# Attention, a polynomial layer and an expert layer on one core: the keys' and queries' work of the pair two on queued behind the reciprocal

## The chip, the cores and the metric

One core of one Trainium2 chip runs the whole program in one launch. The metric is the device time of one execution in microseconds (us); lower is better. The time before is the median of three runs, 1173.3 us (1172.96 to 1173.52).

## The reference

Four batches of eight heads, 768 positions, 64 numbers a head, float32. Attention sees the first four positions (sinks) and a window of 128 behind each position. Its output goes through two layers in turn.

```python
scores = where(keep, q @ k.T / 8, -1e9)          # keep: sink, or 0 <= i - j < 128
a = exp(scores - max); a = a / (sum(a) + 1e-9)
x = (a @ v) as 3072 x 512                        # heads side by side
h = x @ w_in                                     # 512 -> 2048
g = h if h >= 1, 0 if h <= -1, else (h + 1)**2 / 4
x2 = g @ w_out                                   # 2048 -> 512
logits = x2 @ w_gate                             # 8 experts, 384 tokens each
out[mask_e] = relu(x2[mask_e] @ w1[e]) @ w2[e]   # tokens given out greedily by logit
```

## The kernel before

**Work and stages.** Tokens are cut into 12 blocks of 256 (`NB`), three to a batch, so every third block is a batch's first. A block's attention is done in four pairs of heads. Blocks 0 and 1 take a float32 path (`attn_steps_f32`); blocks 2 to 11, so 40 pairs, take `attn_steps`, in which each operand is split into a high and a low part and multiplied in several passes. Beside the attention of one block runs the first layer of the block before it (`moe1_steps`): 16 steps of 12 matmuls into `hp` (L632), the activation on VectorE (L640, L642), ScalarE (L641, L643) and GpSimd (`gl`, L644), and 12 matmuls into `up` (L657). From some 60 to 780 us both run together; after that come the routing and the experts. A function `Plan` sorts all steps by a due time and traces them in that order; a scheduler then orders each engine's queue, and may issue an instruction earlier than another traced before it when it is ready sooner. Each queue is worked off in order.

**One pair.** In the tracing order of `pipeline` (L598) an iteration does, for the pair called `now`, the one after it (`+`), the pair two on (`*`) and three on (`^`):

```python
"ptrans0 ptrans1 strans +s00 +s01 +norm0 pv0 +s10 +s11 +norm1 "
"*trans_k *trans_q ^load_kq "
"pv1 +split_v +sinks *load_v split"
```

- `scores` (s00 to s11): TensorE multiplies queries and keys (L332 with the queries' low part `ql`, L333 with the high part `sq`); VectorE adds the mask and takes the maximum (L335, two instructions); ScalarE takes the exponential and its row sum (L337, the sum in a second record).
- `norm`: VectorE adds 1e-9 to the sums (L342) and takes the reciprocal (L343); GpSimd multiplies the probabilities `pr` by it (L351; L346 and L348 in a batch's first block).
- `ptrans`: TensorE turns `pr` (L370) into `tp`; ScalarE and VectorE make the high and low part `pt` (L372, L373).
- `pv`: TensorE (L389); ScalarE copies one half of the result (L395), VectorE adds the other into `xa` (L396). `split`: GpSimd adds the two parts of `xa` (L408; L405 in a first block), ScalarE makes `xh` (L409), GpSimd `xl` (L410). With the fourth pair's `xh` and `xl` a block's input is complete, and the matmuls of L632 on that block can start.
- `trans_k`, for the pair two on: VectorE turns the keys in place (L428, called through `turned`), ScalarE copies the high part into `ks` (L300) and VectorE subtracts it (L301), one for each head; VectorE copies the sinks' keys (L305 in a first block, L306).
- `trans_q`, for the pair two on: VectorE turns the queries (L428), ScalarE makes `sq` (L314), VectorE `ql` (L315).
- `load_kq`, for the pair three on: SyncE loads keys and queries (L424) into the buffers that `trans_k` and `trans_q` read.

Keys `kr` and queries `qr`, `ks`, `sq` and `ql` have one buffer each; `pr`, `pt` and `sm` have two.

Of the kernel before, what the change touches and what calls it, by code (L numbers as in the profile page):

```python
# [1 line left out]

# [5 lines left out]
F32 = mybir.dt.float32  # L8
F32R = mybir.dt.float32r
# [3 lines left out]
AF = mybir.ActivationFunctionType  # L13
OP = mybir.AluOpType
# [11 lines left out]
P = 128  # L26
NT = S // P
NS = 32
# [46 lines left out]
class Kernel:  # L75
# [174 lines left out]
    def attn_steps(self, blk, xt):  # L250

        nc, a = self.nc, self.a
        pairs = []
        b, t0 = blk // BB, 2 * (blk % BB)
        first = t0 == 0
        kts = [0, 1] if first else [t0 - 1, t0, t0 + 1]
        nk = len(kts)
        for p in range(H // 2):
            st = {}
# [34 lines left out]
            half = [(slice(64 * hh, 64 * hh + 64), slice(64 - 64 * hh, 128 - 64 * hh)) for hh in range(2)]  # L294

            def trans_k(p=p, st=st):
                ks = st["ks"] = self.at.tile([P, 2, 3, W], F32R, name="ks", tag="ks")
                ps = self.turned(st["k"][:, :4 * nk].rearrange("p n c -> p (n c)")).rearrange("p (t c) -> p t c", c=P)
                for hh, (hs, os) in enumerate(half):
                    nc.scalar.copy(ks[hs, hh, :nk, :P], ps[hs])  # L300
                    nc.vector.tensor_tensor(out=ks[os, hh, :nk, :P], in0=ps[hs], in1=ks[hs, hh, :nk, :P].bitcast(F32),  # L301
                                            op=OP.subtract)
                if first:
                    self.sk[p] = self.kp.tile([P, 2, NS], F32R, name="sk", tag=f"sk{p}")
                    nc.vector.tensor_copy(self.sk[p], ks[:, :, 0, :NS].bitcast(F32))  # L305
                nc.vector.tensor_copy(ks[:, :, :nk - 1, P:],  # L306
                                      self.sk[p].bitcast(F32).unsqueeze(2).to_broadcast([P, 2, nk - 1, NS]))

            def trans_q(st=st):
                sq = st["sq"] = self.at.tile([P, 2, 2, P], F32R, name="sq", tag="sq")  # L310
                ql = st["ql"] = self.at.tile([P, 2, 2, P], F32R, name="ql", tag="ql")
                x = self.turned(st["q"].rearrange("p h n c -> p (h n c)"))
                flat = lambda t: t.rearrange("p h u q -> p (h u q)")
                nc.scalar.activation(flat(sq), x, AF.Copy, scale=0.125)  # L314
                nc.vector.scalar_tensor_tensor(flat(ql), x, 0.125, flat(sq).bitcast(F32), op0=OP.mult, op1=OP.subtract)  # L315

            def scores(hh, u, st=st):
                t = t0 + u
# [21 lines left out]
            def norm(hh, st=st):  # L340
                pr, sm = st["pr"][:, :, :, hh], st["sm", hh]
                nc.vector.tensor_scalar(sm[:, 2], sm[:, 1], 1e-9, None, op0=OP.add)  # L342
                nc.vector.reciprocal(sm[:, 2], sm[:, 2])  # L343
                r = sm[:, 2]
                if first:
                    nc.gpsimd.tensor_tensor(out=pr[:, 0, W:], in0=pr[:, 0, W:], in1=r[:, 0:1].to_broadcast([P, P]),  # L346
                                            op=OP.mult)
                    nc.gpsimd.tensor_tensor(out=pr[:, 1], in0=pr[:, 1], in1=r[:, 1:2].to_broadcast([P, 2 * P + NS]),  # L348
                                            op=OP.mult)
                else:  # L350
                    nc.gpsimd.tensor_tensor(out=pr, in0=pr, in1=r.unsqueeze(2).to_broadcast([P, 2, 2 * P + NS]),  # L351
                                            op=OP.mult)
# [45 lines left out]
            def split(p=p, st=st):  # L398
# [7 lines left out]
                else:  # L406
# [4 lines left out]

            pairs.append(dict(
                load_kq=load_kq, load_v=load_v, trans_k=trans_k, trans_q=trans_q,
                split_v=vsplit, sinks=sinks if first else None, strans=None if first else strans, split=split,
                **{f"s{hh}{u}": lambda hh=hh, u=u, f=scores: f(hh, u) for hh in range(2) for u in range(2)},
                **{f"{nm}{hh}": lambda hh=hh, f=f: f(hh) for hh in range(2)
                   for nm, f in (("norm", norm), ("ptrans", ptrans), ("pv", pv))}))
        return pairs

    def load_blocks(self, t, src, ts):  # L420

        for j in range(2):
            blocks = src[ts[0] * P:(ts[-1] + 1) * P, 32 * j:32 * j + 32].rearrange("(n s) d -> s n d", s=32)
            self.nc.sync.dma_start(t[32 * j:32 * j + 32, :4 * len(ts)], blocks)  # L424

    def turned(self, x):

        self.nc.vector.transpose(x, x)  # L428
        return x
# [946 lines left out]
def tile_sink_window_attention__moe__expert_choice(ctx, tc, q, k, v, n_sink, window, w_in, w_out, wg, w1, w2, out):  # L1376
    a = dict(q=q, k=k, v=v, n_sink=n_sink, window=window, w_in=w_in, w_out=w_out, wg=wg, w1=w1, w2=w2, out=out)
    nc = tc.nc
    K = Kernel(ctx, tc, a)
# [3 lines left out]
    xg = dr.tile([B * H * S, D], F32, name="xg")  # L1383
    K.logits = K.c.tile([P, B * NT, E], F32, name="logits")
    K.sk, K.sv, K.skf, K.svf = {}, {}, {}, {}

    def pipeline(general):
        with ExitStack() as c0:
            c1, c3, c4, cd = (c0.enter_context(ExitStack()) for _ in range(4))
            K.pools(c1.enter_context, c0.enter_context)  # L1390
# [72 lines left out]
            plan.run()  # L1463

    pipeline(False)
    flag = nc.values_load(K.flag[0:1, 0:1], min_val=0, max_val=1)
    with tc.If(flag):
        with ExitStack() as c0:
            K.attn_general(c0.enter_context, xg)
        pipeline(True)  # L1470
# [32 lines left out]
```

## Time and profile before

| | |
|---|---|
| profiled execution | 1172.83 us, of which the span of the profile is 1171.0 us |
| median of the runs | 1173.3 us |
| TensorE (PE) busy | 1102.2 us, 94% of the span |
| VectorE (DVE) busy | 872.2 us, 74% |
| ScalarE (ACT) busy | 698.2 us, 60% |
| GpSimd (POOL) busy | 487.0 us, 42% |
| granted TensorE clock, mean | 0.982 of full |

The profile is one execution. An engine's busy time leaves out register, branch, semaphore and DMA-issuing instructions. Matmuls are pipelined, so a busy TensorE is not one at its peak. In a row in order of time stand the start, the duration, the engine, the line of the kernel, the operation, the tiles written and read, their shapes, the count, and in brackets the engine's idle time before it and what ended it. A wait for several things is put down to the last of them.

### The profile page before, as it was taken

What the parts mean: (1) busy time and instruction counts of PE and PEld (TensorE: products, weight loads), DVE (VectorE), ACT (ScalarE), POOL (GpSimd) and SP (SyncE); (2) the same over time, 40 slices, a digit from 0 to 9 for tenths busy, and PEclk for the clock granted to TensorE, in tenths of its full rate; (3) what the DMA queues carried; (4) which work ended last, traced back from release to release, by engine and by line L of the source; (5) the groups of instructions that cost most, each with busy time, mean ns of one, the idle gap of its engine ahead of it and who ended that gap; (6) DMA issues with size and microseconds to landing.
All of it is one profiled execution on the core that took longest, in us unless ns stands there. A gap on an engine that the chain in (4) does not pass through costs nothing.

```text
span 1171.0 us, 24367 instructions
## 1 busy us (share of the span) xinstructions
PE 1102.2 (94%) x8256; PEld 1017.4 (87%) x8256; DVE 872.2 (74%) x2718; ACT 698.2 (60%) x1598; POOL 487.0 (42%) x590
## 2 busy tenths in 40 slices
PE   5899888999999999999999999999799999999997
PEld 3688878999999999999999999999587788788896
DVE  5978978777777877776777787755788888788430
ACT  4887777566666666676667676643245445444552
POOL 1335745444545545455545554542213213322321
PEclk9899999999999999999999999999799999999999
DMA  4645522323222222223222222100485767667772
GB/s 105 173 143 158 158 60 61 70 42 64 53 39 56 36 55 49 61 46 64 34 54 49 58 46 56 22 19 1 120 228 168 204 180 216 188 194 202 217 218 66
DMA packets 241928, 118.13 MB, mean 101 GB/s; under 512 B 196096, under 2 KB 220672, under 8 KB 241792
## 3 DMA queue, kind: packets, MB, share of 16 engines
q1 hardware_dynamic: 231504, 85.36, 28.4%
q0 software_dynamic: 8592, 29.89, 10.9%
q8 instruction: 67, 1.10, 0.4%
q10 hardware_dynamic: 1696, 1.22, 0.3%
q14 instruction: 69, 0.57, 0.2%
HBM read 86.00 MB, written 13.11 MB: 85 GB/s over the span
## 4 chain that ended last, share of the span: by engine, by line
PE 42%; DVE 13%; issue 9%; ACT 6%; POOL 5%; DMA 4%; SPq 2%; DVEq 0%; POOLq 0%; ACTq 0%
PE hp L632 11%; PE up L657 11%; PE hp L1048 6%; PE us L1075 6%; PE xp L389 1%; DVE oh L945 1%; ACT pr L337 1%; ACT u L641 1%; PE tp L370 1%; SPq L424 1%; DVE u L640 1%; DVE ind L801 1%; DVE ks L301 1%; DMA qr<-in_q_dram 1%; POOL gl L644 1%
## 5 line engine op out<-in xcount | busy, mean ns | idle before, releaser
L644 POOL TENSOR_TENSOR gl<-u,gh 128x256 fp32r<-128x256 f32 x192 | 149.5, 779 | 205.3 <-ACT gh L643 169.5
L657 PE MATMUL up<-woh,gl 128*128 128x256 f32 x576 | 166.6, 289 | 2.6 <-POOL gl L644 2.6
L657 PE MATMUL up<-woh,gh 128*128 128x256 f32 x576 | 163.7, 284 | 0.0
L657 PE MATMUL up<-wol,gh 128*128 128x256 f32 x576 | 163.5, 284 | 0.0
L641 ACT ACTIVATE u<-u,half 128x256 f32<-128x256 f32 x192 | 97.4, 508 | 83.4 <-DVE u L640 79.4
L632 PE MATMUL hp<-xh,wil 128*128 128x256 f32 x768 | 132.0, 291 | 3.6 <-ACT xh L409 2.8
L632 PE MATMUL hp<-xl,wih 128*128 128x256 f32 x768 | 126.4, 284 | 2.0 <-POOL xl L410 1.6
L632 PE MATMUL hp<-xh,wih 128*128 128x256 f32 x768 | 124.7, 283 | 0.0
L632 PEld LDWEIGHTS hp<-xh,wil 128*128 128x128 f32 x768 | 107.6, 191 | 5.7 <-ACT xh L409 4.2
L657 PEld LDWEIGHTS up<-woh,gl 128*128 128x128 f32 x576 | 108.9, 189 | 3.2 <-POOL gl L644 3.1
L632 PEld LDWEIGHTS hp<-xl,wih 128*128 128x128 f32 x768 | 106.4, 191 | 3.4 <-POOL xl L410 3.4
L657 PEld LDWEIGHTS up<-wol,gh 128*128 128x128 f32 x576 | 108.6, 189 | 0.4 <-issue 0.4
L657 PEld LDWEIGHTS up<-woh,gh 128*128 128x128 f32 x576 | 108.5, 188 | 0.4 <-issue 0.4
L632 PEld LDWEIGHTS hp<-xh,wih 128*128 128x128 f32 x768 | 106.3, 191 | 0.0
L642 DVE TENSOR_TENSOR u<-hp,u 128x256 f32<-128x256 f32 x192 | 80.5, 420 | 31.6 <-ACT u L641 29.8
L640 DVE TENSOR_SCALAR u<-hp 128x256 f32<-128x256 f32 x192 | 79.9, 416 | 31.0 <-PE hp L632 22.5
L351 POOL TENSOR_TENSOR pr<-pr,sm 128x576 f32<-128x576 f32 x56 | 71.3, 1273 | 67.9 <-DVE sm L343 30.3
L643 ACT CAST gh<-u 128x256 fp32r<-128x256 f32 x192 | 77.6, 404 | 30.3 <-DVE u L642 28.0
L337 ACT ACTIVATE pr<-pr,sm 128x288 f32<-128x288 f32 (+1 forms) x160 | 85.2, 533 | 16.3 <-DVE sm L335 15.7
L1056 ACT ACTIVATE hh<-hp 128x384 fp32r<-128x384 f32 x64 | 31.5, 492 | 102.1 <-PE hp L1048 89.4
L373 DVE TENSOR_TENSOR pt<-tp,pt 128x512 fp32r<-128x512 f32 (+1 forms) x80 | 51.3, 647 | 43.9 <-ACT pt L372 43.4
L1075 PE MATMUL us<-w2h,hl 128*128 128x512 f32 x192 | 80.8, 421 | 0.0
(264 smaller groups left out, 3040.0 us busy)
## 6 DMA issues: line engine op xcount, KB each, us to landing
w1r<-in_moe_w_dram SPq DMA_DIRECT2D x32, 512.0 KB, 4.7
w2r<-in_moe_w_dram SPq DMA_DIRECT2D x32, 512.0 KB, 4.5
w2l<-w2r POOLq DMA_DIRECT2D x32, 512.0 KB
qr<-in_q_dram SPq DMA_DIRECT2D x320, 32.0 KB, 1.9
dr<-in_moe_w_in_dram SPq DMA_DIRECT2D x15, 512.0 KB, 4.1
dr<-in_moe_w_out_dram SPq DMA_DIRECT2D x15, 512.0 KB, 3.7
x2d<-ev SPq DMA_DIRECT2D x26, 256.0 KB, 2.2
vr<-in_v_dram SPq DMA_DIRECT2D x56, 96.0 KB, 2.3
```

What stands on the lines that cost most here:

```text
L337: nc.scalar.activation(pr, pr, AF.Exp, bias=sm[:, 0, u:u + 1], scale=-1.0, accum_out=sm[:, 1, u:u + 1])
L351: nc.gpsimd.tensor_tensor(out=pr, in0=pr, in1=r.unsqueeze(2).to_broadcast([P, 2, 2 * P + NS]), op=OP.mult)
L373: nc.vector.tensor_tensor(out=pt[:, 1, :n], in0=ps, in1=pt[:, 0, :n].bitcast(F32), op=OP.subtract)
L632: nc.tensor.matmul(ps, w_[:, k, fs], x_[:, k, :], start=(i == 0 and k == 0), stop=(i == 2 and k == 3))
L640: nc.vector.tensor_scalar(u, ps, -1.0, 1.0, op0=OP.max, op1=OP.min)
L641: nc.scalar.activation(u, u, AF.Square, bias=self.half, scale=0.5)
L642: nc.vector.tensor_tensor(out=u, in0=ps, in1=u, op=OP.max)
L643: nc.scalar.copy(gh, u)
L644: nc.gpsimd.tensor_tensor(out=gl, in0=u, in1=gh.bitcast(F32), op=OP.subtract)
L657: nc.tensor.matmul(o, g_[:, ts], self.w_out_part(w_, f)[:, cs], start=(f == fa and i == 0 and (cs.start > 0 or t == 0)), stop=(f == fz - 1 ...
L1048: nc.tensor.matmul(ps, w_[:, k, fs], x_[:, k, :], start=(i == 0 and k == 0), stop=(i == 2 and k == 3))
L1075: nc.tensor.matmul(us[j], h_[:, o], w_[:, f % 2, :], start=(f == 0 and i == 0), stop=(f == nf - 1 and i == 2))
```

## The change

A helper, `behind_shares`, opens a block in which every instruction traced for VectorE gets an order edge to the last reciprocal of `norm` traced so far (`self.shares`). Such an edge fixes the order of issue on that engine's queue and waits for nothing else. `trans_k` opens the block after the keys' transposition, `trans_q` around everything. By the tracing order that reciprocal is the one of the next pair's second head (`+norm1`), traced right before. ScalarE's instructions in the block get no edge. The instructions are the same in kind and number. The float32 path does not change.

```diff
--- before.py
+++ after.py
@@ -1,4 +1,4 @@
-from contextlib import ExitStack
+from contextlib import ExitStack, nullcontext
 
 import concourse.bass as bass
 import concourse.tile as tile
@@ -296,23 +296,26 @@
             def trans_k(p=p, st=st):
                 ks = st["ks"] = self.at.tile([P, 2, 3, W], F32R, name="ks", tag="ks")
                 ps = self.turned(st["k"][:, :4 * nk].rearrange("p n c -> p (n c)")).rearrange("p (t c) -> p t c", c=P)
-                for hh, (hs, os) in enumerate(half):
-                    nc.scalar.copy(ks[hs, hh, :nk, :P], ps[hs])
-                    nc.vector.tensor_tensor(out=ks[os, hh, :nk, :P], in0=ps[hs], in1=ks[hs, hh, :nk, :P].bitcast(F32),
-                                            op=OP.subtract)
-                if first:
-                    self.sk[p] = self.kp.tile([P, 2, NS], F32R, name="sk", tag=f"sk{p}")
-                    nc.vector.tensor_copy(self.sk[p], ks[:, :, 0, :NS].bitcast(F32))
-                nc.vector.tensor_copy(ks[:, :, :nk - 1, P:],
-                                      self.sk[p].bitcast(F32).unsqueeze(2).to_broadcast([P, 2, nk - 1, NS]))
+                with self.behind_shares():
+                    for hh, (hs, os) in enumerate(half):
+                        nc.scalar.copy(ks[hs, hh, :nk, :P], ps[hs])
+                        nc.vector.tensor_tensor(out=ks[os, hh, :nk, :P], in0=ps[hs], in1=ks[hs, hh, :nk, :P].bitcast(F32),
+                                                op=OP.subtract)
+                    if first:
+                        self.sk[p] = self.kp.tile([P, 2, NS], F32R, name="sk", tag=f"sk{p}")
+                        nc.vector.tensor_copy(self.sk[p], ks[:, :, 0, :NS].bitcast(F32))
+                    nc.vector.tensor_copy(ks[:, :, :nk - 1, P:],
+                                          self.sk[p].bitcast(F32).unsqueeze(2).to_broadcast([P, 2, nk - 1, NS]))
 
             def trans_q(st=st):
                 sq = st["sq"] = self.at.tile([P, 2, 2, P], F32R, name="sq", tag="sq")
                 ql = st["ql"] = self.at.tile([P, 2, 2, P], F32R, name="ql", tag="ql")
-                x = self.turned(st["q"].rearrange("p h n c -> p (h n c)"))
                 flat = lambda t: t.rearrange("p h u q -> p (h u q)")
-                nc.scalar.activation(flat(sq), x, AF.Copy, scale=0.125)
-                nc.vector.scalar_tensor_tensor(flat(ql), x, 0.125, flat(sq).bitcast(F32), op0=OP.mult, op1=OP.subtract)
+                with self.behind_shares():
+                    x = self.turned(st["q"].rearrange("p h n c -> p (h n c)"))
+                    nc.scalar.activation(flat(sq), x, AF.Copy, scale=0.125)
+                    nc.vector.scalar_tensor_tensor(flat(ql), x, 0.125, flat(sq).bitcast(F32),
+                                                   op0=OP.mult, op1=OP.subtract)
 
             def scores(hh, u, st=st):
                 t = t0 + u
@@ -340,7 +343,7 @@
             def norm(hh, st=st):
                 pr, sm = st["pr"][:, :, :, hh], st["sm", hh]
                 nc.vector.tensor_scalar(sm[:, 2], sm[:, 1], 1e-9, None, op0=OP.add)
-                nc.vector.reciprocal(sm[:, 2], sm[:, 2])
+                self.shares = nc.vector.reciprocal(sm[:, 2], sm[:, 2]).ins
                 r = sm[:, 2]
                 if first:
                     nc.gpsimd.tensor_tensor(out=pr[:, 0, W:], in0=pr[:, 0, W:], in1=r[:, 0:1].to_broadcast([P, P]),
@@ -422,6 +425,10 @@
         for j in range(2):
             blocks = src[ts[0] * P:(ts[-1] + 1) * P, 32 * j:32 * j + 32].rearrange("(n s) d -> s n d", s=32)
             self.nc.sync.dma_start(t[32 * j:32 * j + 32, :4 * len(ts)], blocks)
+
+    def behind_shares(self):
+
+        return self.tc.issue_after(self.shares) if self.shares else nullcontext()
 
     def turned(self, x):
 
@@ -1383,8 +1390,10 @@
     xg = dr.tile([B * H * S, D], F32, name="xg")
     K.logits = K.c.tile([P, B * NT, E], F32, name="logits")
     K.sk, K.sv, K.skf, K.svf = {}, {}, {}, {}
+    K.shares = None
 
     def pipeline(general):
+        K.shares = None
         with ExitStack() as c0:
             c1, c3, c4, cd = (c0.enter_context(ExitStack()) for _ in range(4))
             K.pools(c1.enter_context, c0.enter_context)
```

Below, the issue order at three places, before and in the change. The line numbers in the change are higher: L343 became L346, L342 L345, L301 L302, L306 L307, L305 L306, L315 L317, L335 L338, L428 L435, L396 L399, L373 L376, L640 L647, L642 L649, L590 L597, L351 L354, L644 L651, L408 L411, L410 L413.

VectorE around the second reciprocal of the last pair but one of the last block (at 744 us of the profile), before:

```order
L335 ISA pr,sm<-sc,m_109 128x288
L335 ISA sm 128x1
L301 TENSOR_TENSOR ks<-kr,ks 64x3x128
L642 TENSOR_TENSOR u<-hp,u 128x256
L306 CAST ks<-sk 128x2x2x32
L342 TENSOR_SCALAR sm<-sm 128x2
L428 STREAM_TRANSPOSE qr<-qr 128x512
L343 RECIPROCAL sm<-sm 128x2
L301 TENSOR_TENSOR ks<-kr,ks 64x3x128
L396 TENSOR_TENSOR xa<-xp,xa 64x512
L315 SCALAR_TENSOR_TENSOR ql<-qr,sq 128x512
L373 TENSOR_TENSOR pt<-tp,pt 128x512
```

and in the change:

```order
L338 ISA pr,sm<-sc,m_109 128x288
L338 ISA sm 128x1
L649 TENSOR_TENSOR u<-hp,u 128x256
L345 TENSOR_SCALAR sm<-sm 128x2
L346 RECIPROCAL sm<-sm 128x2
L302 TENSOR_TENSOR ks<-kr,ks 64x3x128 x2
L307 CAST ks<-sk 128x2x2x32
L435 STREAM_TRANSPOSE qr<-qr 128x512
L399 TENSOR_TENSOR xa<-xp,xa 64x512
L376 TENSOR_TENSOR pt<-tp,pt 128x512
L317 SCALAR_TENSOR_TENSOR ql<-qr,sq 128x512
L647 TENSOR_SCALAR u<-hp 128x256
```

Both subtractions of the keys (`ks<-kr,ks`), the copy of the sinks and the queries' transposition stand behind the reciprocal; the step into the reciprocal follows `u` directly. `ql` stands behind the first `pt`.

GpSimd at the same place; the second row of the multiplication of `pr` is the one that this reciprocal releases. Before:

```order
L644 TENSOR_TENSOR gl<-u,gh 128x256 x2
L351 TENSOR_TENSOR pr<-pr,sm 128x576
L644 TENSOR_TENSOR gl<-u,gh 128x256 x2
L351 TENSOR_TENSOR pr<-pr,sm 128x576
L408 TENSOR_TENSOR xa<-xa 128x2x128
L287 TENSOR_TENSOR v_11277<-vr,v_11277 128x6x64
L410 TENSOR_TENSOR xl<-xa,xh 128x256
```

and in the change:

```order
L651 TENSOR_TENSOR gl<-u,gh 128x256 x2
L354 TENSOR_TENSOR pr<-pr,sm 128x576
L651 TENSOR_TENSOR gl<-u,gh 128x256
L354 TENSOR_TENSOR pr<-pr,sm 128x576
L651 TENSOR_TENSOR gl<-u,gh 128x256
L287 TENSOR_TENSOR v_11068<-vr,v_11068 128x6x64
L411 TENSOR_TENSOR xa<-xa 128x2x128
L413 TENSOR_TENSOR xl<-xa,xh 128x256
```

One `gl` that stood ahead of that multiplication now stands behind it, and a split of V (`v<-vr,v`, under its buffer's number) stands ahead of the sum of `xa`.

VectorE around the second reciprocal of the first pair of a batch's third block (at 449 us), before:

```order
L335 ISA pr,sm<-sc,m_108 128x288
L335 ISA sm 128x1
L306 CAST ks<-sk 128x2x2x32
L301 TENSOR_TENSOR ks<-kr,ks 64x3x128 x2
L640 TENSOR_SCALAR u<-hp 128x256
L342 TENSOR_SCALAR sm<-sm 128x2
L343 RECIPROCAL sm<-sm 128x2
L428 STREAM_TRANSPOSE qr<-qr 128x512
L642 TENSOR_TENSOR u<-hp,u 128x256
L396 TENSOR_TENSOR xa<-xp,xa 64x384
L315 SCALAR_TENSOR_TENSOR ql<-qr,sq 128x512
L373 TENSOR_TENSOR pt<-tp,pt 128x384
```

and in the change:

```order
L338 ISA pr,sm<-sc,m_108 128x288
L338 ISA sm 128x1
L647 TENSOR_SCALAR u<-hp 128x256
L345 TENSOR_SCALAR sm<-sm 128x2
L346 RECIPROCAL sm<-sm 128x2
L302 TENSOR_TENSOR ks<-kr,ks 64x3x128 x2
L649 TENSOR_TENSOR u<-hp,u 128x256
L307 CAST ks<-sk 128x2x2x32
L435 STREAM_TRANSPOSE qr<-qr 128x512
L399 TENSOR_TENSOR xa<-xp,xa 64x384
L376 TENSOR_TENSOR pt<-tp,pt 128x384
L317 SCALAR_TENSOR_TENSOR ql<-qr,sq 128x512
```

The copy of the sinks and both subtractions moved from ahead of the reciprocal to behind it, and `xa` and `pt` now stand ahead of `ql`.

VectorE around the second reciprocal after the last pair of a block (at 590 us), before:

```order
L335 ISA pr,sm<-sc,m_108 128x288
L335 ISA sm 128x1
L301 TENSOR_TENSOR ks<-kr,ks 64x2x128 x2
L305 CAST sk<-ks 128x64
L342 TENSOR_SCALAR sm<-sm 128x2
L306 CAST ks<-sk 128x2x32
L640 TENSOR_SCALAR u<-hp 128x256
L343 RECIPROCAL sm<-sm 128x2
L315 SCALAR_TENSOR_TENSOR ql<-qr,sq 128x512
L642 TENSOR_TENSOR u<-hp,u 128x256
L396 TENSOR_TENSOR xa<-xp,xa 64x512
```

and in the change:

```order
L338 ISA pr,sm<-sc,m_108 128x288
L338 ISA sm 128x1
L345 TENSOR_SCALAR sm<-sm 128x2
L346 RECIPROCAL sm<-sm 128x2
L647 TENSOR_SCALAR u<-hp 128x256
L302 TENSOR_TENSOR ks<-kr,ks 64x2x128 x2
L649 TENSOR_TENSOR u<-hp,u 128x256
L306 CAST sk<-ks 128x64
L435 STREAM_TRANSPOSE qr<-qr 128x512
L307 CAST ks<-sk 128x2x32
L399 TENSOR_TENSOR xa<-xp,xa 64x512
L317 SCALAR_TENSOR_TENSOR ql<-qr,sq 128x512
```

Ahead of `xa` stood `ql` and one `u` after the reciprocal; now two `u`, both subtractions, both copies and the queries' transposition stand there.

## Rows read from the trace of the kernel before

**Rows 1.** Table of waits, TensorE, 220 to 780 us: us in total, times, longest.

```profile
PE tp L370 <- POOL pr L351: 12.7, 10, 2.0
PE hp L632 <- ACT xh L409: 2.8, 5, 1.5
PE hp L632 <- POOL xl L410: 1.6, 2, 1.2
PE tp L370 <- POOL pr L346: 1.0, 1, 1.0
PE tp L370 <- POOL pr L348: 0.7, 2, 0.5
```

**Rows 2.** In order of time, 743.9 to 748 us: start, duration, engine, line, operation.

```profile
744.01 0.18 ACT L337 ACTIVATION_READ_ACCUMULATOR pr<-pr,sm 128x1 f32 x1
...
744.20 0.22 DVE L306 CAST ks<-sk 128x128 fp32r<-128x128 f32 x1
...
744.60 0.71 DVE L428 STREAM_TRANSPOSE qr<-qr 128x512 f32<-128x512 f32 x1
...
745.24 0.12 DVE L343 RECIPROCAL sm<-sm 128x2 f32<-128x2 f32 x1
745.29 0.74 POOL L644 TENSOR_TENSOR gl<-u,gh 128x256 fp32r<-128x256 f32 x1 [3.10 <-issue]
...
745.99 1.47 POOL L351 TENSOR_TENSOR pr<-pr,sm 128x576 f32<-128x576 f32 x1
...
747.51 0.75 PE L370 MATMUL tp<-ident,pr 128*128 128x128 f32 x4 [1.07 <-POOL pr L351]
```

**Rows 3.** In order of time, 295.1 to 300.1 us.

```profile
295.11 0.19 ACT L337 ACTIVATION_READ_ACCUMULATOR pr<-pr,sm 128x1 f32 x1
...
295.53 0.17 DVE L343 RECIPROCAL sm<-sm 128x2 f32<-128x2 f32 x1
...
295.73 0.55 DVE L301 TENSOR_TENSOR ks<-kr,ks 64x384 fp32r<-64x384 f32 x1
...
295.84 1.47 POOL L351 TENSOR_TENSOR pr<-pr,sm 128x576 f32<-128x576 f32 x1 [1.18 <-DVE sm L343]
...
296.57 1.15 DVE L301 TENSOR_TENSOR ks<-kr,ks 64x384 fp32r<-64x384 f32 x1 [0.29 <-ACT ks L300]
...
297.75 1.12 DVE L315 SCALAR_TENSOR_TENSOR ql<-qr,sq 128x512 fp32r<-128x512 f32 x1
```

**Rows 4.** In order of time, 447.6 to 453 us.

```profile
447.74 0.19 ACT L337 ACTIVATION_READ_ACCUMULATOR pr<-pr,sm 128x1 f32 x1
...
448.95 0.17 DVE L343 RECIPROCAL sm<-sm 128x2 f32<-128x2 f32 x1
...
449.96 0.39 DVE L642 TENSOR_TENSOR u<-hp,u 128x256 f32<-128x256 f32 x1
...
450.38 0.55 DVE L396 TENSOR_TENSOR xa<-xp,xa 64x384 f32<-64x384 f32 x1
...
450.96 0.69 DVE L315 SCALAR_TENSOR_TENSOR ql<-qr,sq 128x512 fp32r<-128x512 f32 x1
...
452.80 0.29 PE L332 MATMUL sc<-ks,ql 128*128 128x288 f32 x1
...
452.95 0.56 DVE L373 TENSOR_TENSOR pt<-tp,pt 128x384 fp32r<-128x384 f32 x1 [1.29 <-ACT pt L372]
```

**Rows 5.** In order of time, 588.9 to 594.6 us.

```profile
589.00 0.19 ACT L337 ACTIVATION_READ_ACCUMULATOR pr<-pr,sm 128x1 f32 x1
...
591.31 0.68 DVE L396 TENSOR_TENSOR xa<-xp,xa 64x512 f32<-64x512 f32 x1 [0.18 <-ACT xa L395]
...
592.54 0.73 POOL L408 TENSOR_TENSOR xa<-xa 128x256 f32<-128x256 f32 x1
...
593.76 0.39 PE L632 MATMUL hp<-xh,wil 128*128 128x256 f32 x1 [0.39 <-ACT xh L409]
```

**Rows 6.** Busy time by engine (PE PEld DVE ACT POOL), clock, DMA, 640 to 660 us.

```profile
640.00:660.00 20.00, 18.01 (x137) 17.82 (x136) 14.39 (x41) 12.07 (x31) 8.53 (x10) 0.91 0.32 73
```

## The prediction

> **What bounds the kernel now.** I read the table of waits first, for TensorE alone and for the stretch from 220 to 780 us, in which attention of one block runs beside the first expert layer of the block before it [rows 1]. TensorE is hardly ever free there, so what it waits for is what a change of order can give or take. The longest item is the transposition of the probabilities (L370), which waits for GpSimd's normalisation (L351): 10 waits, 12.7 us. With the same wait on the two instructions of a batch's first block (L346 and L348: 1.0 and 0.7 us) that is 14.4 us. Next come the first matmuls of a block (L632), which wait for the split of the attention output (L409, L410): 2.8 and 1.6 us. No score matmul waits for the queries in this stretch. Then I read the instructions of all engines in order of time at four places.
>
> At 744 us [rows 2] the reader sees how the first wait arises. The row sums of the last exponential are out at 744.19 (ScalarE, L337). VectorE had by then begun on the keys of the pair two on, and puts the transposition of the queries (0.71 us) between the two steps of the reciprocal, which ends at 745.36, 1.17 us after its input. GpSimd takes a `gl` first (745.29, 0.74 us), then the normalisation, 745.99 to 747.46, and TensorE stands for 1.07 us until 747.51. At 295 us [rows 3] nothing stood between: row sums at 295.30, reciprocal done at 295.70. So 0.40 us is the shortest way from the sums to their reciprocal.
>
> **The change, part by part.** It adds and removes no instruction; all of it is order. VectorE's two subtractions (L301) and copies (L305, L306) for the keys, and the transposition (L428) and low part (L315) for the queries, now stand behind the reciprocal. The issue order shows this in each of the pairs, and at 744 us GpSimd's normalisation also stands ahead of the `gl`.
>
> *A, what goes.* At 744 us the reciprocal would end at 744.19 + 0.40 = 744.59 and the normalisation begin about 0.14 later (295.84 after 295.70 in [rows 3]), at 744.73 in place of 745.99. That is 1.26 us, more than the wait of 1.07, so the whole wait goes. I did the same for each wait of [rows 1] on L346, L348 and L351, capped by how much earlier its normalisation can be. Four of these 14.4 us of waits, 4.9 us together, lie in the last pair of a block, right ahead of a wait for `xh`; they are counted under C. The other 9.5 us give up 7.7 by my estimate.
>
> *B, what the moved work costs the scores.* The moved instructions used VectorE's time while ScalarE was still at the exponential. Now they come after it, and the next pair's first scores (L332) need `ql`, the last of them. They also run at the same time as the normalisation, and that has a price which [rows 3] show, since the two subtractions stood behind the reciprocal there too: the first took 0.55 us, the second 1.15, the normalisation 1.47, and the low part of the queries, beside the next GpSimd instruction, 1.12 in place of the 0.69 at 450.96 in [rows 4]. From reciprocal to the end of the second subtraction 2.02 us passed, where twice 0.55 would be 1.10. The Trainium skill (SBUF — State Buffer, Who interferes with whom) has a rule on this: a VectorE instruction with two SBUF inputs and a GpSimd instruction that reads SBUF share one read port, and the one that comes second is blocked for the whole of the other. By that rule the two subtractions with the normalisation between them would take 0.55 + 1.15 + 0.55 = 2.25 us, 0.23 more than the row, and the eight late pairs below would cost 1.8 us more; I go by the row.
>
> The pair at 449 us [rows 4] is worked out in full. Row sums at 447.93, reciprocal at 448.33; then the subtractions 2.02, `u` of the expert layer (L642) 0.39, the sink copy (L306, 0.22 in [rows 2]), the queries' transposition 0.71 [rows 2], `xa` (L396) 0.55, the first low part of the probabilities (L373) 0.56, and `ql` 0.69 to 1.12. Sum 5.14 to 5.57: `ql` at 453.5 to 453.9. The scores start at 452.80 now, so they would wait 0.7 to 1.1 us. Before, `ql` was done at 451.65, 1.15 us early. I did this for all 40 pairs, each from its own rows. In most, `ql` is 2 to 3 us early now and just holds. In eight it comes late, by 0.3 to 2.0 us, 8.5 us together. With every instruction at its duration alone the eight cost 3. I take 8.5, because [rows 3] are the nearest rows there are, and keep 3 as the other end.
>
> *C, the block's end.* After the last pair of a block TensorE already waits for `xh`. At 589 us [rows 5]: row sums at 589.19, `xa` done at 591.99, GpSimd's sum of the halves (L408) 592.54 to 593.27, `xh` behind it, and the matmul starts at 593.76 after 0.39 us of waiting. In the changed order `xa` stands behind the subtractions, both copies and the queries' transposition: 589.59 and some 3.8 us, so 593.4, and L408 starts 0.85 later than now. A wait saved shortly before is then waited here. Eight such places, each worked out so, come to between -0.8 and +1.4 us and to +2.0 together. GpSimd's new order (the split of V ahead of this sum in some) is in it. At the uncontended durations they give -2.6: 0.9 less at most of them.
>
> *The rest.* The loads of the next keys and queries start when these buffers are read, so later by as much as B; they land 1.4 us or more before their use now, most by over 3, and I cost this at nothing; if that cover is gone, VectorE stands at L428 with everything behind it. Between 150 and 220 us the issue order changes on TensorE too. Waits on L351 and on `ql` there are some 4 us, and I put the stretch at 0, between -2 and +2. After 780 us nothing moves but the start.
>
> Sum: -7.7 + 8.5 + 2.0 = +2.8 us. The profiled execution took 1172.8 us, so 1175.6. It lies 0.5 below the median of the runs, 1173.3. On the median the forecast is **1176 us**, a little slower.
>
> **The rivals.** *The cover holds, faster:* VectorE and GpSimd get in each other's way less than at 295 us, since the normalisation and the first subtraction do not always start together. Then -7.7 + 3.0 - 2.6 = -7.3, or 1166 us. For it: `ql` is early by more than 2 us in most pairs, and no score waits for it from 220 us on [rows 1]. Against it: [rows 3], where the second subtraction and the low part of the queries took 0.6 and 0.4 us more than alone. It decides where the surcharge of 0.9 us a pair falls under about a third of itself. *The two cancel:* two thirds of that surcharge gives -7.7 + 6.7 + 0.5 = -0.5, or 1173 us, which a measurement of this kernel does not tell from no change (0.2%, 2.3 us). *Slower still, by the clock:* after the longest wait of all the granted clock in the stretch from 640 to 660 us was 0.91 of the full [rows 6], that is 20 us with 3.6 of them at 1.2 instead of 2.4 GHz, some 1.8 us lost. Where three of the new waits of 1 us and more do that, the time is 2.8 + 5 more, 1181 us. For it: a wait of 1.5 to 2 us is at the height of those before such a fall. Against it: the longest old waits go, and their fall with them.
>
> **How the numbers follow.** The forecast (slower by 0.2 to 0.5%) has 0.37 and slower by the clock 0.10, so slower 0.47. The two cancel: 0.25. The cover holds: 0.28. The range takes the forecast's own bounds and reaches down to the faster case's middle and up to the clock's: 1166 to 1181.
>
> **What would show it.** In the profile after: waits of L370 on the normalisation from 220 us on down from 14.4 us to under 7; the score matmuls (L332, there L335) waiting for `ql` by some 8 us where there was none; the normalisation's median up from its present length alone, and the second subtraction near 1.1 us in most pairs; waits for `xh` and `xl` not smaller than 4.4 us. If the waits on L370 fall and no wait for `ql` appears, the forecast is wrong and the first rival right. If the waits on L370 stay, step A is wrong: then something other than the reciprocal's place held the normalisation.

## The result, and the profile after

The change takes **1187.4 us** (median of six runs, 1185.0 to 1190.1) where the kernel before takes 1173.3: ratio 1.0119, 95% interval 1.0099 to 1.0139. The forecast was 1176 with a range of 1166 to 1181. The direction was right, the size was not: +14 us in place of +2.8, and outside the range. The profiled execution took 1189.5 us, 16.7 more than the one before.

The busy time of the engines (the page's first part; before it was 1102.2 us for TensorE and 872.2 for VectorE):

```profile
PE 1111.2 (94%) x8256; PEld 1021.0 (86%) x8256; DVE 899.3 (76%) x2718; ACT 701.7 (59%) x1598; POOL 492.2 (41%) x590
```

VectorE has the same 2718 instructions and is busy for 27 us more. Then the table of waits, TensorE, 220 to 790 us (total, times, longest), which answers to [rows 1]:

```profile
PE hp L639 <- ACT xh L412: 14.4, 8, 2.6
PE sc L335 <- DVE ql L317: 3.5, 5, 1.0
PE sc L335 <- DVE pt L376: 3.0, 5, 1.0
PE tps L363 <- DVE xa L399: 1.9, 6, 0.6
PE hp L639 <- POOL xl L413: 0.8, 4, 0.2
PE tp L373 <- POOL pr L354: 0.2, 1, 0.2
```

The 14.4 us of waits on the normalisation have all but gone. In their place stand 8.4 us ahead of the scores and of the transposition of the probabilities' middle part (L363), and the waits on `xh` rose from 2.8 to 14.4 us, now at every one of eight block ends.

Third, VectorE's own waits from 220 to 775 us, two rows each, before:

```profile
DVE pt L373 <- ACT pt L372: 42.4, 39, 2.3
...
DVE sm L342 <- ACT pr L337: 13.0, 20, 0.7
```

and in the change:

```profile
DVE sm L345 <- ACT pr L340: 23.4, 30, 1.8
...
DVE pt L376 <- ACT pt L375: 2.0, 5, 0.6
```

VectorE now stands 10 us longer waiting for the exponential, with the keys' work held back behind the reciprocal. It pays for that later: before, it was ready ahead of ScalarE for 39 of the `pt` and waited 42 us for them; now it waits 2 us. The `pt`, `xa` and `ql` have become VectorE's lateness.

The block end that the prediction worked out [rows 5] lies at 599 us in the change (in order of time: start, duration, engine, line):

```profile
599.01 0.19 ACT L340 ACTIVATION_READ_ACCUMULATOR pr<-pr,sm 128x1 f32 x1
599.24 0.17 DVE L345 TENSOR_SCALAR sm<-sm 128x2 f32<-128x2 f32 x1 [1.81 <-ACT pr L340]
599.44 0.17 DVE L346 RECIPROCAL sm<-sm 128x2 f32<-128x2 f32 x1
...
599.98 1.23 DVE L302 TENSOR_TENSOR ks<-kr,ks 64x256 fp32r<-64x256 f32 x2
...
601.24 0.42 DVE L649 TENSOR_TENSOR u<-hp,u 128x256 f32<-128x256 f32 x1
601.58 0.18 DVE L306 CAST sk<-ks 128x64 fp32r<-128x64 f32 x1
601.68 0.70 DVE L435 STREAM_TRANSPOSE qr<-qr 128x512 f32<-128x512 f32 x1
...
602.24 0.73 POOL L651 TENSOR_TENSOR gl<-u,gh 128x256 fp32r<-128x256 f32 x1 [1.31 <-issue]
...
602.31 0.71 DVE L307 CAST ks<-sk 128x64 fp32r<-128x64 f32 x1
...
603.05 0.68 DVE L399 TENSOR_TENSOR xa<-xp,xa 64x512 f32<-64x512 f32 x1
...
603.81 1.23 POOL L411 TENSOR_TENSOR xa<-xa 128x256 f32<-128x256 f32 x1 [0.85 <-DVE xa L399]
...
605.53 0.58 PE L639 MATMUL hp<-xh,wil 128*128 128x256 f32 x1 [2.64 <-ACT xh L412]
```

VectorE idles for 1.81 us, does the reciprocal at once (0.41 us after the row sums), and then has 3.4 us of work ahead of `xa`. GpSimd, which waited for nothing but `xa` here (0.85 us), passes that on to `xh` and TensorE.

**Where the 16.7 us lie.** The first layer's 37th step starts 1.8 us later than before (238.0 against 236.2 us), its 181st 15.7 us later (799.5 against 783.8); the last 1.0 us falls behind that. Between the two I counted TensorE's lost time from the start of each matmul to the start of the next, what exceeds its streaming time by over 0.1 us. This is more than the table of waits gives, because a matmul of 0.28 us is followed by the next after 0.12, so that the first 0.16 us of a wait lie beside it and shorter waits don't appear. By what released TensorE:

| us lost, 37th to 181st step | before | change |
|---|---|---|
| transposition on the normalisation, away from block ends (A) | 10.5 | 1.0 |
| scores on `ql` (B) | 0 | 4.5 |
| scores on `pt`, L363 on `xa` (B) | 0.2 | 11.2 |
| block ends: `xh`, `xl`, and waits on the normalisation shortly ahead (C) | 13.5 | 19.2 |
| clock at 1.2 GHz in 220 to 790 us: half of that time | 3.4 | 6.8 |

The rows differ by 15.1 us together, 1.2 more than the 13.9 of this stretch; some of the time at 1.2 GHz lies in waits.

### The profile page after: what moved, and what is told of

The parts are those of the page before. It is cut to its first block, busy times and chain, and to the rows that moved or that the text cites. A ratio compares the mean times of both kernels' runs of the same rounds, so it can differ in the third digit from the quotient of the medians.

```text
span 1187.7 us, 24356 instructions
## 1 busy us (share of the span) xinstructions
PE 1111.2 (94%) x8256; PEld 1021.0 (86%) x8256; DVE 899.3 (76%) x2718; ACT 701.7 (59%) x1598; POOL 492.2 (41%) x590
## 4 chain that ended last, share of the span: by engine, by line
PE 54%; DVE 24%; issue 7%; ACT 6%; DMA 4%; SPq 2%; POOL 2%; ACTq 0%; DVEq 0%; POOLq 0%
PE hp L639 15%; PE up L664 13%; PE hp L1055 8%; PE us L1082 7%; DVE ks L302 3%; DVE xa L399 2%; PE xp L392 2%; DVE qr L435 2%; SPq L427 2%; DVE u L647 2%; ACT pr L340 1%; DVE df L244 1%; DVE oh L952 1%; PE sc L335 1%; DVE ks L307 1%
## 5 line engine op out<-in xcount | busy, mean ns | idle before, releaser
L651 POOL TENSOR_TENSOR gl<-u,gh 128x256 fp32r<-128x256 f32 x192 | 151.0, 787 | 200.3 <-ACT gh L650 185.5
L639 PE MATMUL hp<-xh,wil 128*128 128x256 f32 x768 | 132.5, 291 | 15.1 <-ACT xh L412 14.4
L639 PE MATMUL hp<-xl,wih 128*128 128x256 f32 x768 | 126.8, 285 | 0.9 <-POOL xl L413 0.8
L639 PE MATMUL hp<-xh,wih 128*128 128x256 f32 x768 | 125.6, 285 | 0.0
L639 PEld LDWEIGHTS hp<-xh,wil 128*128 128x128 f32 x768 | 107.5, 191 | 17.8 <-ACT xh L412 16.1
L647 DVE TENSOR_SCALAR u<-hp 128x256 f32<-128x256 f32 x192 | 80.6, 420 | 45.1 <-PE hp L639 37.0
L649 DVE TENSOR_TENSOR u<-hp,u 128x256 f32<-128x256 f32 x192 | 80.6, 420 | 37.6 <-ACT u L648 36.0
L639 PEld LDWEIGHTS hp<-xl,wih 128*128 128x128 f32 x768 | 107.2, 192 | 2.2 <-POOL xl L413 2.2
L639 PEld LDWEIGHTS hp<-xh,wih 128*128 128x128 f32 x768 | 107.2, 193 | 0.0
L354 POOL TENSOR_TENSOR pr<-pr,sm 128x576 f32<-128x576 f32 x56 | 71.9, 1284 | 64.4 <-ACT ks L301 30.8
L340 ACT ACTIVATE pr<-pr,sm 128x288 f32<-128x288 f32 (+1 forms) x160 | 85.1, 533 | 14.2 <-DVE sm L338 13.4
L1082 PE MATMUL us<-w2h,hh 128*128 128x512 f32 x192 | 75.6, 394 | 0.0
```

The source lines that it names most:

```text
L340: nc.scalar.activation(pr, pr, AF.Exp, bias=sm[:, 0, u:u + 1], scale=-1.0, accum_out=sm[:, 1, u:u + 1])
L639: nc.tensor.matmul(ps, w_[:, k, fs], x_[:, k, :], start=(i == 0 and k == 0), stop=(i == 2 and k == 3))
L647: nc.vector.tensor_scalar(u, ps, -1.0, 1.0, op0=OP.max, op1=OP.min)
L649: nc.vector.tensor_tensor(out=u, in0=ps, in1=u, op=OP.max)
L651: nc.gpsimd.tensor_tensor(out=gl, in0=u, in1=gh.bitcast(F32), op=OP.subtract)
L1082: nc.tensor.matmul(us[j], h_[:, o], w_[:, f % 2, :], start=(f == 0 and i == 0), stop=(f == nf - 1 and i == 2))
```

## The experiments

All ratios are to the kernel before, run on the same chip in turn.

| run | us | ratio, 95% interval |
|---|---|---|
| `xa` first at the block's end | 1171.6 | 0.9981 (0.9970 to 0.9991) |
| block's end alone | 1190.0 | 1.0132 (1.0109 to 1.0155) |
| all but the block's end | 1176.4 | 1.0023 (1.0013 to 1.0033) |
| fourth pair's work alone | 1173.6 | 1.0004 (0.9987 to 1.0021) |
| change with the wait filled | 1183.1 | 1.0078 (1.0061 to 1.0095) |
| `xa` first everywhere | 1192.5 | 1.0153 (1.0132 to 1.0174) |
| keys' part alone | 1190.6 | 1.0152 (1.0132 to 1.0172) |
| **queries' part alone** | **1162.7** | **0.9905 (0.9888 to 0.9921)** |
| change, half the normalisation | 1176.5 | 1.0014 (1.0000 to 1.0028) |
| before, half the normalisation | 1158.7 | 0.9855 (0.9829 to 0.9881) |
| queries' part, V's split behind the sum | 1163.9 | 0.9899 (0.9875 to 0.9924) |
| queries' part and the sinks' copies | 1161.4 | 0.9897 (0.9880 to 0.9914) |

### Where in the block: four runs

**`xa` first at the block's end.** Where the current pair is a block's fourth, the edge that holds the keys and queries leads to `ins`, the addition into `xa`:

```diff
+                if hh == 1 and p == 3 and blk > 2:
+                    self.shares = ins.ins
...
-  "*trans_k *trans_q ^load_kq pv1 +split_v ..."
+  ("pv1 *trans_k *trans_q ^load_kq " if n % 4 == 3 else "*trans_k *trans_q ^load_kq pv1 ") + "+split_v ..."
```

> The change, with one difference: in the last pair of a block the keys' and queries' work of the pair two on is queued behind the addition into xa (L399) too, instead of ahead of it. TensorE's queue is the same as in the change. Theory 1 (block's end): the waits for xh cost the time, because xa stands behind two subtractions, two copies and the queries' transposition. Then the waits of L639 on xh from 220 to 790 us fall from 14.4 to 1 to 4 us and the time from 1187 to 1172 to 1177 us. Theory 2 (scores): the late queries and late low parts of the probabilities in all pairs cost it; then the time stays at 1184 to 1190 us whatever xh does.

Measured: 1171.6 us, just under the expected, and 16 less than the change, by `xa` passing some 2 to 3.5 us of VectorE's work at eight places (it ends 1.1 to 2.6 us after the row sums there, in the change 4.5 to 4.8). Waits of TensorE, 220 to 795 us (two lines lower are the numbers of L639 and L412 here):

```profile
PE hp L641 <- ACT xh L414: 4.7, 5, 1.6
PE sc L335 <- DVE ql L317: 3.4, 4, 1.0
PE sc L335 <- DVE pt L376: 3.0, 5, 1.0
```

The waits of the scores are those of the change; those on `xh` fell (14.4 to 4.7, where 1 to 4 were expected), and with them went the stretches at the lower clock: none between 220 and 790 us, where the change had 13.7 us at 1.2 GHz. Theory 2 fails.

**The end alone, and all but the end.** The edge only for the work of a block's second pair (traced with the fourth pair of the block before), or for all other pairs: `self.behind_shares(p == 1)` and `self.behind_shares(p != 1)`.

> The change only where it falls on a block's last pair (the work for each block's second pair); all other pairs as before. Theory 1 (block's end): waits for xh rise by some 10 us and some 5 us of waits on the normalisation go; with the falls of the clock that follow the longest waits 1177 to 1184 us. Theory 2 (scores): nearly nothing is left of the loss, 1170 to 1174 us.

> The change in all pairs except a block's last one (there the work for the block's second pair is free as before). Theory 1 (block's end): the loss is gone; some 9 us of waits on the normalisation go and some 6 to 8 us of waits of the scores come, so 1170 to 1176 us. Theory 2 (scores): the loss stays, 1183 to 1188 us.

Measured: 1190.0 and 1176.4 us. The end alone costs even more than the whole change: its waits on the normalisation stay (13.2 us, 10 times), and those on `xh` come on top (220 to 795 us):

```profile
PE tp L373 <- POOL pr L354: 13.2, 10, 1.9
PE hp L639 <- ACT xh L412: 10.5, 6, 2.2
```

In 220 to 790 us the clock fell to a half five times (17.1 us, 8.5 lost). Without the end no clock fall is left in this stretch, and some 2 us of loss remain, just above what theory 1 gave. The two parts don't add up (+15.8 and +2.2 against +14.1).

**The fourth pair's work alone**, `self.behind_shares(p == 3)`:

> The change only for the work of each block's fourth pair, which stands behind the reciprocal of its third pair. In the kernel before the normalisation of that third pair held TensorE for 9 us in the middle of six blocks. Theory 1 (block's end) and the working of the prediction (A and B weighed pair by pair): these 9 us go, at most 4 us of waits of the fourth pair's scores come, 1167 to 1171 us. Theory 2 (scores): each queued pair costs more than it gives, a quarter of the loss stays, 1175 to 1179 us.

Measured: 1173.6 us, which is no change; a miss for both theories. The waits it aimed at shrank as expected, but later in the chain others came: from start to start A fell by 5.7 us and B rose by 7.7; that no clock fall is left in this stretch (3.4 us before) makes up for it. One wait of a microsecond became several of 0.3 to 1.

### The clock

**The wait filled.** Ten transpositions in front of the matmuls that wait for `xh`:

```diff
+            if f == 0 and blk > 2:
+                for _ in range(10):
+                    nc.tensor.transpose(ps[:, :P], self.ident, self.ident)
```

> The change, with ten more transpositions of the identity (1.2 us at the spacing of the other transpositions) on TensorE right ahead of the first matmuls of each block from the fourth on, into the bank that these overwrite. TensorE then works through most of its wait for xh. Theory 1 with a part for the clock: the ends of the waits do not move, but the granted clock no longer falls to a half at or after the block ends (475 and 605 us of the change); 1182 to 1185 us, 3 to 5 us less than the profiled run of the change. If the clock has no part in the loss: 1186 to 1191 us, with the falls still there or without effect.

Measured: 1183.1 us, as expected with the clock. Each row is a stretch of 20 us: busy time by engine (PE PEld DVE ACT POOL), granted clock, DMA, in the change:

```profile
600.00:620.00 20.00, 17.36 (x122) 17.16 (x121) 13.79 (x40) 10.84 (x30) 7.64 (x11) 0.83 0.23 55
470.00:490.00 20.00, 18.33 (x138) 17.86 (x138) 14.55 (x37) 11.72 (x29) 8.69 (x11) 0.91 0.27 62
```

and at the same places with the wait filled:

```profile
596.00:616.00 20.00, 18.68 (x155) 18.28 (x155) 15.86 (x46) 11.73 (x32) 9.13 (x14) 1.00 0.26 60
466.00:486.00 20.00, 19.43 (x161) 19.02 (x160) 15.90 (x41) 13.01 (x32) 10.65 (x12) 1.00 0.30 71
```

With TensorE at work through the wait the clock stays at 2.4 GHz from 220 to 790 us. The profiled runs differ by 6.8 us (1189.5 and 1182.7), which is the half of the 13.7 us that the change spent at 1.2 GHz there; 5.9 of the 6.8 lie between the 37th and the 181st step of the first layer. The other runs of the change lie at 1185 us, with a mean granted clock of 0.981, and at 1189 to 1190 us, with 0.979 as in the profiled one, so probably not every execution falls as often. The rest of the loss is the waits themselves.

### Which work

**Keys alone, queries alone**, with `self.behind_shares(False)` in `trans_q` or in `trans_k`:

> Only the keys' part of the change: the subtractions and copies behind the reciprocal, the queries' transposition and low part free as before. Theory 1 (queue ahead of xa at the block's end): the waits for xh lie between, 9 to 13 us, and the time at 1179 to 1185 us. Theory 3 (VectorE's subtractions and GpSimd's normalisation at the same time slow each other down, and that is the loss): all of it stays, 1185 to 1190 us.

> Only the queries' part of the change: their transposition and low part behind the reciprocal, the keys' subtractions and copies free as before. Theory 1: the queries' transposition (0.7 us) now stands ahead of xa where it did not, xh waits rise by 2 to 5 us, and a part of the waits on the normalisation goes: 1173 to 1179 us. Theory 3 (the subtractions beside the normalisation): no loss, 1170 to 1174 us.

Measured: 1190.6 and **1162.7 us**. The first lies just above what theory 3 gave, though its waits on `xh` are those of theory 1; the second lies far below every expectation: one half of the change is worth -11.5 us, the other costs 16.5, more than the whole. Keys' part (220 to 795 us):

```profile
PE hp L639 <- ACT xh L412: 12.9, 8, 2.7
PE tps L363 <- DVE xa L399: 9.6, 9, 1.3
```

and queries' part, TensorE's waits and, in a fence of their own, VectorE's for `pt` and for the exponential:

```profile
PE hp L639 <- ACT xh L412: 2.9, 3, 1.7
PE sc L335 <- DVE pt L376: 2.7, 5, 1.3
PE hp L639 <- POOL xl L413: 2.1, 6, 0.5
PE tp L373 <- POOL pr L354: 1.5, 3, 0.7
PE sc L335 <- DVE ql L317: 1.3, 4, 0.7
```

```profile
DVE pt L376 <- ACT pt L375: 25.0, 30, 1.6
...
DVE sm L345 <- ACT pr L340: 9.5, 17, 0.7
```

The waits on the normalisation go in both (1.2 and 1.5 us left). But where the keys' work is free, it fills the time in which VectorE waits for the exponential anyway (9.5 us of such waits, where the change has 23.4), and the rest of the queue stays early. What had stood between the sums and the reciprocal, and was worth moving, is by [rows 2] the queries' transposition; it and the low part were not run apart.

**Contention or queue?** A third theory was that the keys' work costs because it now runs beside the normalisation. Both kernels with half the normalisation left out (in a batch's first block its first instruction):

```diff
-  nc.gpsimd.tensor_tensor(out=pr, in0=pr, in1=r.unsqueeze(2).to_broadcast([P, 2, 2 * P + NS]), op=OP.mult)
+  nc.gpsimd.tensor_tensor(out=pr[:, 1], in0=pr[:, 1], in1=r[:, 1:2].to_broadcast([P, 2 * P + NS]), op=OP.mult)
```

> The change, with GpSimd's normalisation left out for the first 128 rows of each block (only the second half of the probabilities is divided by its sum), so that it takes some 0.67 us instead of 1.3. To be read against the kernel before with the same half left out. If the loss comes mostly from the simultaneous use of VectorE and GpSimd (contention), the mean of the keys' subtractions (64x384) falls from 875 to 650 to 750 ns, the copies of the sinks (128x128) from 628 to under 450, xa ends some 4.0 us after the row sums at a block's end instead of 4.6, and the change is only 4 to 8 us slower than the kernel before with the same half left out. If it comes from the length of the queue alone, the difference between the two stays at 11 to 15 us.

> The kernel before, with GpSimd's normalisation left out for the first 128 rows of each block. The base for the run on the change with the same half left out. The transposition's waits on the normalisation (14.4 us) become shorter by up to 0.6 us each; 1163 to 1170 us under either theory.

Groups of VectorE's instructions, 220 to 775 us (count, total us, mean ns, idle ahead), the subtraction before:

```profile
L301 DVE TENSOR_TENSOR ks<-kr,ks 64x384 fp32r<-64x384 f32 x48 | 31.8, 662 | 4.4 <-ACT ks L300 3.1
```

in the change, with the copy:

```profile
L302 DVE TENSOR_TENSOR ks<-kr,ks 64x384 fp32r<-64x384 f32 x48 | 42.0, 875 | 1.4
...
L307 DVE CAST ks<-sk 128x128 fp32r<-128x128 f32 x24 | 15.1, 628 | 0.5
```

and in the change with half the normalisation:

```profile
L302 DVE TENSOR_TENSOR ks<-kr,ks 64x384 fp32r<-64x384 f32 x48 | 33.2, 692 | 1.4
L307 DVE CAST ks<-sk 128x128 fp32r<-128x128 f32 x24 | 15.2, 631 | 0.5
```

The subtraction was back at nearly its old length, and yet the change stood 17.7 us above its base (1176.5 against 1158.7), not 4 to 8, and more than the 11 to 15 of the queue alone. But the two differences are not alike. This base has little left to win back on the normalisation, 3.8 us of waits (220 to 785 us) where the kernel before had 14.4:

```profile
PE tp L368 <- POOL pr L349: 3.2, 7, 1.0
...
PE tp L368 <- POOL pr L346: 0.6, 1, 0.6
```

By these tables, as an estimate, what the change costs beside that gain is some 14.1 + 14.2 = 28 us with the whole normalisation and 17.7 + 3.8 = 21.5 with half of it. At the block ends `xa` still ended 4.2 to 4.5 us after the row sums (4.5 to 4.8 in the change, 2.0 to 2.8 before). So the lengthening of the subtractions is real and not the main cost: three quarters stay without most of it, and theory 1, the place in the queue, is left for them. Whether the last quarter is the lengthening or the shorter normalisation itself, the two runs don't tell. The copies' lengthening did not go away here, so the next run takes them alone.

**Queries' part and the sinks' copies.** The edge around the copies of `trans_k`, not its subtractions:

> The queries' part of the change, and of the keys' part only the copies of the sinks' keys (0.2 to 0.3 us alone) behind the reciprocal; the two subtractions free as before. If what counts is how much of VectorE's work is taken out of the time in which it otherwise stands waiting for the exponential (the subtractions are some 1.1 to 1.3 us of it, the copies 0.3), the time stays near that of the queries' part alone, 1162 to 1167 us. If the copies are the costly part (their mean duration doubles in the change), it is 1172 us or more.

Measured: 1161.4 us, the same as the queries' part alone (the intervals overlap). The copies cost nothing. The change differs from this run by the edge on the two subtractions alone and takes some 26 us more (ratios 1.0119 and 0.9897), so it is the subtractions behind the reciprocal that lose the time.

### Two that missed

**`xa` first everywhere**: the first experiment's edge and order in all pairs.

> The change, with the keys' and queries' work of the pair two on queued behind the addition into xa (L399) in every pair, not only in a block's last one. Theory 1 (the order on VectorE sets the time; what TensorE waits for goes ahead): the waits of the transposition L363 on xa (1.3 us in five places with xa first at the block's end alone) go too, and the time falls to 1168 to 1171 us. Theory 2 (queries and keys late): ql moves behind xa in every pair, the waits of the scores on ql rise from 3.4 us to 6 or more and the time is 1173 to 1179 us.

Measured: 1192.5 us. The scores wait 24.2 us for `ql`, far beyond theory 2, and the waits on L363 are gone (220 to 795 us):

```profile
PE sc L335 <- DVE ql L317: 24.2, 22, 2.0
```

But the order also moved the float32 path's value product, and the first layer already starts 7.1 us late there (39.0 against 31.9 us), so some 7 of the 18 us are not about `xa`.

**V's split behind the sum**, on top of the queries' part:

> Only the queries' part of the change, and at a block's end GpSimd's split of V queued behind its sum into xa. In the run with the queries' part alone 5.0 us of waits on xh and xl were left at the block ends from 220 us on, in three of which the split of V stood between the sum and xl. If what TensorE waits for at a block's end sets the time there, the waits on xl (2.1 us) halve and the time is 1159 to 1162 us; if the split of V is itself needed soon, the scores' and the value product's matmuls wait instead and it stays at 1162 to 1164 us.

Measured: 1163.9 us, no gain. The time is that of the second alternative, but not its waits: the scores wait for `pt` 3.0 us (2.7 with the queries' part alone) and for `ql` 1.3 (the same), while the waits on `xl` rose from 2.1 to 4.2 us. What holds `xl` there is left open.

## Why the prediction was right in direction and wrong in size

Two terms of the sum failed, B and C. With the clock they account for the miss: of the 13.9 us between forecast and profiled run B is 7.0, C 3.7 and the clock, for which the sum had nothing, 3.4; A took 1.8 off, 2.8 came outside the counted stretch, and 1.2 are counted twice. That the change would be slower had a chance of 0.47 in the forecast, so the direction was no firm call.

- **A (-7.7): right.** The waits on the normalisation went, and a little more of them (10.5 to 1.0 us away from the block ends, from start to start).
- **B (+8.5): mis-sized, +15.5.** `ql` itself was late by less than I took (4.5 us). What I left out stands next to it in VectorE's queue: I priced the moved work by its last instruction, and not by `pt` and `xa`, which I had counted among the things ahead of `ql`. TensorE waits for these two as well, 11.2 us in 23 short waits. (By the code the scores and L363 write banks that `pt` and `xa` read last; no run tested this.)
- **C (+2.0): mis-sized, +5.7,** and with the falls of the clock, all three of which follow a block's end, the step on which the loss hangs. At the worked place I had `xa` 4.2 us after the row sums; it was 4.53. I had GpSimd's sum start 0.85 later than before; it was 1.26 later, took 1.23 us in place of 0.73, and TensorE arrived 0.49 us earlier, counted from the row sums: together the 2.25 us by which the wait grew (0.39 to 2.64). That the waits removed upstream let TensorE arrive sooner was in my working as a wait "saved shortly before"; at this place none had been saved just ahead, and TensorE had this lead already when the sums came out. The runs with `xa` first there (16 us less) and without the end (11 less) show that at most some 2 us of loss are left once the block end is spared, although B stays.
- **The rest (0): some 1.8 us** up to the 37th step. 1.1 of them lie before 140 us, for which I had no term; what falls in the stretch from 150 to 220 us is within the bound of 2.
- **The rival by the clock was half right.** The clock cost 3.4 us more than before, where I gave that case 5 us and a chance of one in ten. The old longest waits did go, but eight new ones of up to 2.6 us took their place.
- **The rival "the cover holds" failed as a whole and was right for one half of the change.** I priced the moved work as one thing. Its two parts have opposite signs: -11.5 us for the queries', +16.5 for the keys'.
- Of the signs named: waits of L370 under 7 us, yes (0.2); `xh` and `xl` not smaller, yes; scores on `ql` by some 8 us, half; the second subtraction near 1.1 us in most pairs, no (of the 24 on 64x384 between 220 and 775 us 15 took 1.40 to 1.43 us and the others 0.66 to 0.95); the normalisation's median up, no (1166 ns on 128x576 where it was 1165).

## What to carry over

An edge that puts work behind an instruction which itself waits can turn the engine's idle time into a delay of all that follows, so before moving work "behind X", ask what the engine does while X waits, and move only what truly stands between X and its input (here the queries' part, worth 11 us). Price the move by every consumer in the queue behind it, among them, by the code, those that only free a PSUM bank, and by the place where a stage ends. A change made of two parts deserves two runs: here the half is 1% faster than the kernel before, and the whole 1.2% slower.

## What the runs showed that I had not expected

A subtraction that meets the normalisation is not slowed but held. At 279 us of the change (in order of time):

```profile
279.54 0.17 DVE L346 RECIPROCAL sm<-sm 128x2 f32<-128x2 f32 x1
279.74 1.99 DVE L302 TENSOR_TENSOR ks<-kr,ks 64x384 fp32r<-64x384 f32 x2
279.85 1.46 POOL L354 TENSOR_TENSOR pr<-pr,sm 128x576 f32<-128x576 f32 x1 [1.56 <-ACT xa L398]
...
282.10 0.60 DVE L307 CAST ks<-sk 128x128 fp32r<-128x128 f32 x1
...
282.62 0.70 DVE L435 STREAM_TRANSPOSE qr<-qr 128x512 f32<-128x512 f32 x1
...
282.75 0.73 POOL L651 TENSOR_TENSOR gl<-u,gh 128x256 fp32r<-128x256 f32 x1
```

The first subtraction took 0.55 us, as alone. The second began during the normalisation and ended at 281.73, 0.42 us after it (281.31). From the reciprocal's end to there 2.02 us passed, as in [rows 3]: the price that the prediction went by held here. A copy of the sinks took 0.71 us at 602.31 us of the change and ended 0.05 us after GpSimd's `gl` (602.97); the same copy in the kernel before:

```profile
589.60 0.20 DVE L306 CAST ks<-sk 128x64 fp32r<-128x64 f32 x1
```

The transposition of the queries took 0.70 beside a `gl`, as before. The Trainium skill (SBUF — State Buffer, Who interferes with whom) says that the engine which comes second is blocked for the whole of the other's instruction, and that VectorE's copies and casts can be among those concerned. These rows agree but for 0.13 us: held to the end of the normalisation, the second subtraction would have ended 0.55 us after it, not 0.42.

That a fall of the clock in one stretch can be kept off by idle transpositions in a wait was expected as a test, not as a gain: it gave back 4 us of the median (1187.4 to 1183.1).
